# Rebuilding the stretch between a kernel's last lag products and its first feed-forward: first segments first, the first norm in halves, weights fetched apart

## The chip, the cores and the metric

One core of a Trainium2 chip runs the kernel. The metric is the device time of one execution in microseconds. The kernel before was timed three times: 1184.76, 1185.22 and 1189.84 us, median 1185.22 us.

## The reference, cut to what matters

Two layers, each a long convolution over time (a state-space model, S4) and a SwiGLU feed-forward part, each with a layer norm ahead of it and a residual around it. 2048 time steps, 512 channels, 128 states per channel, 1376 hidden columns, all in float32.

```python
def _A_ref(u, ...):                                  # the convolution
    P = jnp.exp(logdA[:, :, None] * l[None, None, :])
    K = jnp.einsum("dn,dnl,dn->dl", Cc, P, dB).real  # a kernel of 2048 lags for each channel
    ...                                              # y = K * u by FFT, + u * Dskip
def _B_ref(x, w_gate, w_up, w_down):
    g = _silu(x @ w_gate)
    u = x @ w_up
    return (g * u) @ w_down
x = A_u
x = x + _A_ref(_layernorm(x), ...)
x = x + _B_ref(_layernorm(x), ...)
x = x + _A_ref(_layernorm(x), ...)
x = x + _B_ref(_layernorm(x), ...)
```

## The kernel before, in words

Time is cut into four blocks of 512 steps. A block's convolution is done by transforms of short segments: the input block is turned into spectra in four groups of frequencies (`q`, in the order 0, 3, 1, 2, and in two halves `h` of 256 channels each), each spectrum is multiplied by the spectrum of a segment of the lags, products of earlier blocks with later segments are added up, and the result is turned back. The kernel runs in two stages.

**The lag kernel.** The lags are built for 64 channels at a time, in eight chunks. For a chunk the vector engine (DVE) builds tables of powers, TensorE (PE) multiplies them (`lags`, L510 and L511), spreads the result over the rows (`spread`, L526), and turns each of its four segments into spectra (`spectra`, matmuls on L547). Segment 0 alone goes into `w0r`, which stays in SBUF. Segments 1 to 3 need a sum of a segment with the other part of the one before (the wrap sums, tile `wo`) and go to DRAM (`wdr`). The wrap sums of chunks 0 to 5 are written on DVE (`wrapped`, L584 and L586), those of chunks 6 and 7 on GpSimd (POOL, L569, or L572 and L573 where segment 0 came ahead by itself).

**The blocks.** Then come eight pairs of a convolution (`ssm`) and a feed-forward part (`ffn`), in the order (layer, block) 00, 01, 02, 10, 03, 11, 12, 13. In an `ssm`, for each half and each `q`: the products (L762, and L765 adding the next one on), two rows that make a complex result of them (L766, L767), the inverse matmuls (L781, tile `pi`), `combine` (L742, L743), and after the four groups of a half fourteen rows of sums that add the result onto the block's rows `xt` (L796 to L811, many through the helper on L226). An `ffn` takes a block's 512 rows in two halves of 256. For each: the norm (`ffn_norm`), five groups of 256 columns of gate and up products (`pgu`, L886 to L888; SiLU on ScalarE (ACT), L891; product on DVE, L892; split into two f16 parts, L893 and L894), the last 96 columns (`remainder`, L853 to L855, on DVE L862 and L864), then the second product (`py`, L900 to L902), which DVE adds to the two rows of tiles (L905). So each half ends with two DVE rows on L905, the "adds"; the kernel has 32 of them. The norm of every half but the first ends in DVE rows on L839 (tile `nn`), and DMA transposes then bring it to PE.

All products of the feed-forward run with numbers split into two f16 parts, a high and a low one. So the f32 weights are split once: fetched, scaled and rounded to the high part on ACT (`hi`, L652 and L677), and the low part worked out on DVE (`lo`, L658 with 688 or 1376 columns a row, L680 with 512).

**The stretch between.** The change sits between the last chunk's `lags` and the first matmul of the first `ffn`. There the first convolution block has only one segment (`ssm(0, 0)`, generator `first`), its spectra of u wait in `u4`, and the first norm goes by a path of its own: bn_stats on DVE (L202, L203), four small POOL instructions (L204 to L207), a normalization on ACT (L825), eight PE transposes (L827), a high copy on ACT (L830) and a low part on DVE (L832).

What sets the order: the code of the lag kernel, through to the last weight split, stands in a `manual_schedule` block, which keeps PE, ACT and DVE in the order written among themselves. Code behind it (the other `ssm`s and `ffn`s) is placed by a list scheduler with priorities, and it may place later code among the rows of the block. Each engine then executes its own list strictly in order and waits at the first row whose input isn't there. SP issues the DMAs of the weights, of `wdr`, `udr` and the transposes, in order as well.

Of the kernel before, what the change touches and what calls it, by code (L numbers as in the profile page):

```python
# [12 lines left out]
F16 = mybir.dt.float16  # L13
# [3 lines left out]
OP = mybir.AluOpType  # L17
# [64 lines left out]
def kernel(ctx, tc, x, a_re, a_im, b_re, b_im, c_re, c_im, log_dt, d_skip,  # L82
# [449 lines left out]
    def spectra(ch, kt, k0, k1, qs=QORD, late=False):  # L532
# [4 lines left out]
        for q in qs:  # L537
            if k1 == 1:
                pw = pbig([P, 2, 8, 4, 16], "pw")[:, :, 0:1]
            elif k0 == 1:  # L540
                pw = pbig([P, 2, nk, 4, 16], "pw")
            else:
                pw = psml([P, 2, nk, 4, 16], "pw")
# [7 lines left out]
            if k1 == 1:  # L551
                A.activation(w0r[:, h, q, :, off:off + DC].rearrange("p i (g d) -> p i g d", g=4), pw[:, :, 0], AF.Copy)
                yield
                continue
            s1 = tl([P, 2, NB, 4, 16], "s1", "uu")
            A.activation(s1[:, :, :nk], pw, AF.Copy)
            if late:
                A.activation(w0r[:, h, q, :, off:off + DC].rearrange("p i (g d) -> p i g d", g=4), pw[:, :, 0], AF.Copy)
                wraps.append(wrapped(h, q, off, s1))
                yield  # L560
                continue
            if k0 == 0:
                G.tensor_copy(w0r[:, h, q, :, off:off + DC].rearrange("p i (g d) -> p i g d", g=4), s1[:, :, 0])
            sp, np_ = s1, NB - 1
            wo = tl([P, 2, NB - 1, 4, 16], "wo", "sg")
            ops = (OP.subtract, OP.add) if q % 2 == 0 else (OP.add, OP.subtract)
            for i in range(2):
                if k0 == 0:
                    G.tensor_tensor(wo[:, i], s1[:, i, 1:], s1[:, 1 - i, :3], ops[i])  # L569
                else:  # L570
                    w0s = w0r[:, h, q, 1 - i, off:off + DC].rearrange("p (g d) -> p g d", g=4)
                    G.tensor_tensor(wo[:, i, 0], s1[:, i, 0], w0s, ops[i])  # L572
                    G.tensor_tensor(wo[:, i, 1:], s1[:, i, 1:3], s1[:, 1 - i, :2], ops[i])  # L573
            for k in range(1, NB):
                nc.sync.dma_start(wdr[k, h, q, :, :, off:off + DC].rearrange("p i (g d) -> p i g d", g=4),
                                  wo[:, :, k - 1])
# [606 lines left out]
```

## Time and profile before

| what | value |
|---|---|
| median of three runs | 1185.22 us |
| the profiled execution's own time | 1189.7 us |
| its span | 1187.9 us |
| PE busy | 1108.9 us, 93% of the span |
| DVE busy | 1017.2 us, 86% |
| ACT busy | 621.3 us, 52% |
| POOL busy | 112.9 us, 10% |
| first matmul of the first feed-forward | 324.80 us |
| 2nd, 4th and 6th add (end of the first three halves' work) | 387.65, 446.57, 512.11 us |

"Busy" is the time in which an engine had an instruction under way; matmuls overlap one another, so a busy PE need not be one at its peak. Line numbers are those of the kernel before unless the text says otherwise; names of tiles stand in the form out<-in. The rows "waited for" give idle time of an engine just ahead of an instruction and what ended it. A column PEclk is the clock that TensorE was granted, 1.00 being full speed.

### The profile page before, as it was taken

How to read it: one execution, taken by the hardware profiler on the slowest of the kernel's cores; microseconds unless marked ns; L12 is line 12 of the kernel's file. 1: busy time of each engine (PE TensorE's matmuls, PEld its weight loads, DVE VectorE, ACT ScalarE, POOL GpSimd, SP SyncE). 2: the span in 40 equal slices, each digit the busy share in tenths (PEclk: the TensorE clock that was granted, in tenths of full speed). 3: DMA queues.
4: the chain of work that ended last, by engine and by line, in shares of the span. 5: the costliest groups of instructions: out<-in, count | busy, mean ns of one | idle time of the engine just before them, and what ended most of it. 6: DMA issues, size and time to landing. Idle time of an engine off the chain costs nothing.

```text
span 1187.9 us, 25243 instructions
## 1 busy us (share of the span) xinstructions
PE 1108.9 (93%) x10268; PEld 862.1 (73%) x10268; DVE 1017.2 (86%) x1669; ACT 621.3 (52%) x1190; POOL 112.9 (10%) x166
## 2 busy tenths in 40 slices
PE   2999899889789989899999999999999999999998
PEld 2867677677675848687768687858687686877875
DVE  8979999998899998999999999989992899983211
ACT  6999889862383553538553534735432452334211
POOL 3100200004200010001000100111000010000000
PEclk9989999999899989999999999989999999999999
DMA  6445455577695238332343444324534144312000
GB/s 235 124 139 127 119 124 124 128 191 197 193 282 170 76 115 200 114 103 83 103 151 122 121 167 144 105 77 155 153 105 135 45 121 134 120 41 46 14 23 18
DMA packets 138455, 146.90 MB, mean 124 GB/s; under 512 B 77858, under 2 KB 87074, under 8 KB 138339
## 3 DMA queue, kind: packets, MB, share of 16 engines
q1 hardware_dynamic: 133474, 128.51, 36.0%
q0 software_dynamic: 4864, 16.78, 6.1%
q8 instruction: 80, 1.31, 0.5%
q14 instruction: 37, 0.30, 0.1%
HBM read 98.19 MB, written 28.31 MB: 106 GB/s over the span
## 4 chain that ended last, share of the span: by engine, by line
PE 37%; DVE 24%; issue 4%; ACT 3%; DMA 3%; SPq 1%; POOL 1%; DVEq 0%; ACTq 0%; POOLq 0%
PE pgu L886 5%; PE pgu L887 5%; PE pgu L888 5%; PE py L900 5%; PE py L901 5%; PE py L902 4%; DVE t L762 4%; PE pi L781 3%; DVE yk L765 3%; PE pf L270 3%; DVE z L226 2%; DVE yk L762 2%; DMA mix<-nn 2%; DVE sg L892 2%; DVE hl L894 2%
## 5 line engine op out<-in xcount | busy, mean ns | idle before, releaser
L886 PE MATMUL pgu<-mix,wsl 128*128 128x256 f16 x1280 | 351.1, 274 | 4.6 <-DVE mix L832 2.4
L887 PE MATMUL pgu<-mix,wsl 128*128 128x256 f16 x1280 | 351.1, 274 | 0.0
L888 PE MATMUL pgu<-mix,wsl 128*128 128x256 f16 x1280 | 350.9, 274 | 0.0
L900 PE MATMUL py<-wsl,hh 128*128 128x512 f16 (+1 forms) x352 | 135.4, 385 | 9.3 <-DVE xg L905 4.7
L887 PEld LDWEIGHTS <-wsl 128*128 128x128 f16 x1280 | 125.9, 98 | 22.2 <-issue 5.9
L886 PEld LDWEIGHTS <-wsl 128*128 128x128 f16 x1280 | 126.0, 98 | 16.6 <-issue 0.3
L902 PE MATMUL py<-wsl,hl 128*128 128x512 f16 (+1 forms) x352 | 135.3, 384 | 2.7 <-DVE hl L894 2.7
L888 PEld LDWEIGHTS <-wsl 128*128 128x128 f16 x1280 | 126.0, 98 | 15.4
L901 PE MATMUL py<-wsl,hh 128*128 128x512 f16 x320 | 123.3, 385 | 0.0
L762 DVE TENSOR_TENSOR t<-uu,w 128x1024 f32<-128x1024 f32 x96 | 116.7, 1216 | 0.2
L765 DVE TENSOR_TENSOR yk<-yk,t 128x1024 f32<-128x1024 f32 x96 | 116.6, 1215 | 0.1
L891 ACT ACTIVATE sg<-pgu,sc 128x512 f32<-128x512 f32 x80 | 54.4, 680 | 106.5 <-PE pgu L888 100.2
L892 DVE SCALAR_TENSOR_TENSOR sg<-pgu,sc,sg 128x512 f32<-128x512 f32 x80 | 59.5, 744 | 50.6 <-ACT sg L891 50.4
L781 PE MATMUL pi<-yl,mix 128*128 128x256 f16 x672 | 91.6, 273 | 8.6 <-ACT yl L770 6.8
L547 PE MATMUL pw<-kt,ek 128*128 128x256 f32 (+2 forms) x420 | 95.9, 365 | 0.0
L893 ACT ACTIVATE hh<-sg 128x512 f16<-128x512 f32 x80 | 50.0, 626 | 78.5 <-DVE sg L892 78.3
L547 PEld LDWEIGHTS pw<-kt,ek 128*128 128x128 f32 x420 | 76.3, 190 | 9.1
L270 PE MATMUL pf<-z,eh 128*128 128x256 f16 x576 | 76.0, 273 | 0.0
L770 ACT ACTIVATE yl<-mix,sy 128x512 f16<-128x512 f32 x56 | 40.2, 718 | 64.5 <-DVE mix L767 64.3
L781 PEld LDWEIGHTS <-mix 128*128 128x128 f16 x672 | 65.1, 98 | 12.1 <-issue 2.2
L762 DVE TENSOR_TENSOR yk<-u,w0r 128x1024 f32<-128x1024 f32 x56 | 68.0, 1215 | 0.9 <-ACT u L272 0.9
L901 PEld LDWEIGHTS <-hh 128*128 128x128 f16 (+1 forms) x352 | 34.8, 99 | 46.4 <-issue 11.8
(247 smaller groups left out, 2182.9 us busy)
## 6 DMA issues: line engine op xcount, KB each, us to landing
w<-wdr SPq DMA_DIRECT2D x96, 256.0 KB, 2.7
uu<-udr SPq DMA_DIRECT2D x96, 256.0 KB, 3.0
udr<-u POOLq DMA_DIRECT2D x32, 256.0 KB, 2.5
wdr<-wo SPq DMA_DIRECT2D x96, 64.0 KB, 2.7
udr<-u SPq DMA_DIRECT2D x16, 256.0 KB, 2.2
g<-tmp POOLq DMA_DIRECT2D x8, 512.0 KB, 4.5
g<-btl POOLq DMA_DIRECT2D x8, 512.0 KB, 5.9
n<-xdr SPq DMA_DIRECT2D x4, 1024.0 KB, 5.6
```

Source lines behind the costliest of these rows:

```text
L270: PE.matmul(pf[:, o], lhsT=e, rhs=m, start=k == 0, stop=k == len(terms) - 1)
L547: PE.matmul(pw[:, i], lhsT=e, rhs=kt[:, :, c + 4 * k0:4 * k1:4, :].rearrange("p g k d -> p k g d"), start=c == 0, stop=c == 3)
L762: V.tensor_tensor(t, uu.unsqueeze(1).to_broadcast([P, 2, 2, HD]), w.unsqueeze(2).to_broadcast([P, 2, 2, HD]), OP.mult)
L765: V.tensor_tensor(yk, yk, t, OP.add)
L781: PE.matmul(pi[:, o], lhsT=e, rhs=m, start=k == 0, stop=k == len(terms) - 1)
L886: PE.matmul(o, lhsT=wgu(wi, k, 0)[:, fs], rhs=nh[:, k], start=k == 0, stop=False)
L887: PE.matmul(o, lhsT=wgu(wi, k, 0)[:, fs], rhs=nlo[:, k], start=False, stop=False)
L888: PE.matmul(o, lhsT=wgu(wi, k, 1)[:, fs], rhs=nh[:, k], start=False, stop=k == 3)
L892: V.scalar_tensor_tensor(sg, pgu[:, 1], sc6[:, 4:5], sg, OP.mult, OP.mult)
L900: PE.matmul(py[:, r], lhsT=hh[:n, f, rc], rhs=wd(f, 0)[:n], start=f == 0, stop=False)
L901: PE.matmul(py[:, r], lhsT=hh[:n, f, rc], rhs=wd(f, 1)[:n], start=False, stop=False)
L902: PE.matmul(py[:, r], lhsT=hl[:n, f, rc], rhs=wd(f, 0)[:n], start=False, stop=f == FT - 1)
```

## The change

Four things are rebuilt; the computation is the same.

- **First segments first.** Segment 0's spectra of the last two chunks, which the first convolution block needs, are taken ahead of everything else of these chunks: three groups of chunk 7 with 64 columns, and group 2 of both chunks at once with 128 (`firsts`). The segments 1 to 3 (`rest`: five groups, 192 columns) come later, partly behind the first norm's transposes. All wrap sums are on DVE now (L583, L585), none on POOL, and POOL's copies into `w0r` are ACT's.
- **The first block by itself.** `opening` replaces `ssm(0, 0)`: results, inverses, combines and the sums can be placed one at a time, the sums in three parts (first two output rows, third, fourth). The rows that the first norm doesn't need (third and fourth) come behind it.
- **The first norm in halves.** Statistics are taken on 256 columns of a half as soon as it is summed (L894); scale and offset are worked out on DVE, POOL does only the power (L900 of the change); one of the two rows is normalized on DVE (L905 of the change); transposes, high copies and low parts (L913 to L918) go in two pieces.
- **Weights fetched apart.** The DMA of a weight piece is no longer in its `hi`: a third list, `fetches`, starts them earlier, into more buffers (a tile `spare` in `W3`). w_down comes in pieces of three rows of tiles instead of four. Two pieces' high parts are on ACT before the first block is done.

The first steps of `ssm(0, 1)` are taken within the stretch, and the block with the order written out now ends ahead of the remaining splits, which the list scheduler places.

```diff
-    def ffn_norm(layer, b, s, wait=None):
...
+    def first_norm():
...
+        def half(h):
+            for r in range(rows):
+                V.bn_stats(st[:, r, h], xt[:, r, h * HD:(h + 1) * HD])
+        def scale():
+            for r in range(rows):
+                V.bn_aggr(mv[:, r], st[:, r])
+            V.tensor_scalar(rs[:, :rows], mv[:, :, 1], EPS, 1.0 / 256.0 ** 2, OP.add, OP.mult)
+            G.tensor_tensor(rs[:, :rows], rs[:, :rows], mhalf[:, :rows], OP.pow)
+        def normal():
+            V.scalar_tensor_tensor(nb[:, :rows], mv[:, :, 0], -1.0, rs[:, :rows], OP.mult, OP.mult)
+            A.activation(nn2[:, 0], xt[:, 0], AF.Identity, scale=rs[:, 0:1], bias=nb[:, 0:1])
+            V.tensor_scalar(nn2[:, 1], xt[:, 1], rs[:, 1:2], nb[:, 1:2], OP.mult, OP.add)
...
     spectra (...)
-            ops = (OP.subtract, OP.add) if q % 2 == 0 else (OP.add, OP.subtract)
-            for i in range(2):
-                if k0 == 0:
-                    G.tensor_tensor(wo[:, i], s1[:, i, 1:], s1[:, 1 - i, :3], ops[i])
-                else:
...
+            wraps.append(wrapped(h, q, off, s1, ("bb", "dd")[len(rests) % 2] if k0 else "sg"))
...
-        ready = ffn_norm(0, 0, 0, lambda: split(0, 2))
-        split(1, 0)
-        take(rest, 100)
-        split(1, 0)
-        take(first, 1)
-        split(0, 1)
-        while los:
-            split(1, 1) if his else split(0, 1)
...
+        result(7)
+        fetch(4)
+        for n in range(4, 8):
+            inverse(n)
...
+        sums1[0]()
+        half(1)
+        scale()
+        take(rest, 6)
...
+        normal()
+        flip(0)
+        flip(2)
+        split(2, 0)
+        ahead.append(next(spec))
+        second_block = ssm(*SEQ[1])
+        take(second_block, 1)
+        while wraps and len(wraps) > 3:
+            wrap()
+        sums0[1]()
+        low(0)
+        low(2)
+        split(0, 2)
+    split(2, 2)
+    fetch(2)
+    sums0[2]()
...
+        if k in (0, 2):
+            take(rest, 3)
...
```

How the rows move is seen in the order in which each engine gets its instructions. First PE, from the last spectra of the stretch to the first matmul of the feed-forward (`pw` are spectra of the lags, `pt` the transposed first rows, `pgu` the first feed-forward product). Before:

```order
L547 MATMUL pw<-kt_629,ef 128x192
L547 MATMUL pw<-kt_629,ek_85 128x192 x3
L827 MATMUL pt<-ident,nn_3422 128x128 x8
L886 LDWEIGHTS wsl_3116
L886 MATMUL pgu<-mix,wsl_3116 128x256
```

and now:

```order
L913 MATMUL pt<-ident,nn_3300 128x128 x8
L543 MATMUL pw<-kt_629,ef 128x192
L543 MATMUL pw<-kt_629,ek_84 128x192 x3
L543 MATMUL pw<-kt_629,ef 128x192
L543 MATMUL pw<-kt_629,ek_84 128x192 x3
L543 MATMUL pw<-kt_629,ef 128x192
L543 MATMUL pw<-kt_629,ek_85 128x192 x3
L543 MATMUL pw<-kt_629,ef 128x192
L543 MATMUL pw<-kt_629,ek_85 128x192 x3
L963 LDWEIGHTS wsl_3108
L963 MATMUL pgu<-mix,wsl_3108 128x256
```

Two groups of spectra, sixteen matmuls of 192 columns, now stand between the transposes and the feed-forward.

Second DVE, at the end of the first block's sums and the first statistics (`bn` rows; `wsl` is the split weights, `st` a fetched piece, `xg` the block's rows, `mix` on L832 the normed rows). Before:

```order
L202 BN_STATS st<-xg 128x6
L203 BN_AGGR mv<-st 128x2
L202 BN_STATS st<-xg 128x6
L203 BN_AGGR mv<-st 128x2
L658 SCALAR_TENSOR_TENSOR wsl_3116<-st_3301,sc_93,wsl_3116 128x2x344
L658 SCALAR_TENSOR_TENSOR wsl_3117<-st_3301,sc_93,wsl_3116 128x2x344
L658 SCALAR_TENSOR_TENSOR wsl_3118<-st_3304,sc_93,wsl_3117 128x4x344
L832 TENSOR_TENSOR mix<-pt,mix 128x1024
```

and now:

```order
L806 TENSOR_TENSOR t_3301<-t_3301,t_3302 128x256
L687 SCALAR_TENSOR_TENSOR wsl_3110<-st_3489,sc_93,wsl_3110 128x512
L226 SCALAR_TENSOR_TENSOR xg<-t_3301,xg 128x256
L894 BN_STATS st<-xg 128x6
L687 SCALAR_TENSOR_TENSOR wsl_3110<-st_3489,sc_93,wsl_3110 128x512
L894 BN_STATS st<-xg 128x6
L861 TENSOR_TENSOR dd_2915<-bb_2914,pi 128x512
L862 TENSOR_TENSOR bb_2914<-bb_2914,pi 128x512
```

Low parts of w_down (L687) now stand among the first half's sums, ahead of its statistics; they need the fetch of w_down and its high part. In all, from the end of the table building to the low part of the normed rows, the change has six split rows of 688 columns on DVE where before has two, two of 1376 where before has one, two of 512 where before has none, and ten wrap sums where before has none.

Third DVE around the 4th add, where the second half of the first feed-forward ends (L905 before, L982 now). Before, the normed rows `nn` (L839) of the next feed-forward are made at the 3rd add, well ahead of the 4th:

```order
L839 TENSOR_TENSOR nn_3422<-nn_3422 128x512
L226 SCALAR_TENSOR_TENSOR z_3524<-bt 128x256 x2
L905 SCALAR_TENSOR_TENSOR xg<-py,sc_93,xg 128x512
L226 SCALAR_TENSOR_TENSOR xg<-t_3844,xg 128x256
L226 SCALAR_TENSOR_TENSOR t_3845<-bb,dd 128x256
L765 TENSOR_TENSOR yk<-yk,t 128x1024
L226 SCALAR_TENSOR_TENSOR t_3844<-dd,bb 128x256
L839 TENSOR_TENSOR nn_3422<-nn_3422 128x512
```

and now, a piece that begins with the 4th add:

```order
L982 SCALAR_TENSOR_TENSOR xg<-py,sc_93,xg 128x512
L226 SCALAR_TENSOR_TENSOR z_3540<-z_3540 128x2x256
L762 TENSOR_TENSOR yk<-yk,t 128x1024
L226 SCALAR_TENSOR_TENSOR xg<-t_3859,xg 128x256
L812 TENSOR_TENSOR t_3868<-dd 128x256
L226 SCALAR_TENSOR_TENSOR z_3540<-bt 128x256 x2
L759 TENSOR_TENSOR t<-uu,w 128x1024
L226 SCALAR_TENSOR_TENSOR t_3873<-dd,bb 128x256
L813 TENSOR_TENSOR t_3867<-t_3867,t_3868 128x256
L762 TENSOR_TENSOR yk<-yk,t 128x1024
```

The last sums of block (0, 1) now follow the 4th add, and its normed rows (L877 now) come another nine and sixteen rows behind this piece:

```order
L877 TENSOR_TENSOR nn_3300<-nn_3300 128x512
L226 SCALAR_TENSOR_TENSOR yl_3541<-mix,sy,yl_3541 128x512
L226 SCALAR_TENSOR_TENSOR xg<-t_3873,xg 128x256
L762 TENSOR_TENSOR yk<-yk,t 128x1024
L226 SCALAR_TENSOR_TENSOR z_3540<-z_3540 128x2x256
L759 TENSOR_TENSOR t<-uu,w 128x1024
L226 SCALAR_TENSOR_TENSOR dd<-pi,sy,bb 128x512
L877 TENSOR_TENSOR nn_3300<-nn_3300 128x512
```

Of DVE's rows between the 2nd and the 4th add, the change has fewer than before (1 product, 3 additions of products, 2 `z` and 1 low part of it, 9 sums, 1 low part `yl`, 2 `nn`, 2 of the remainder), and between the 4th and the 6th more (4 products, 5 additions, 2 rows of results, 8 sums, 1 `yl`, 2 `nn`).

More of the change, by code (lines that the diff above doesn't have):

```diff
@@ L1076 @@
         spec, ahead = inputs(), []
-        first = ssm(0, 0)
+        result, inverse, combine, total = opening()
         sp = spectra(i, kt, 0, NB, QORD[:3])
@@ L1110 @@
         scales()
-        take(first, 2)
-        load_x(xs[0], 0, 0)
+        kp = spread(i, ks)
+        inverse(1)
+        combine(0)
+        split(1, 0)
+        A.activation(kts[1], kp, AF.Copy)
+        result(2)
+        wrap()
+        wrap()
+        result(3)
+        sp = itertools.chain(spectra(i, kts[1], 0, 1, QORD[:3]), firsts(i - 1, kt2, QORD[3]))
+        rest = itertools.chain(spectra(i - 1, kts[0], 1, NB, QORD[3:]), spectra(i, kts[1], 1, NB))
+        split(0, 1)
         take(sp, 2)
-        take(first, 2)
```

295 lines of the change are left out of this document (184 added, 111 removed).

## The prediction

> **What bounds the kernel now.** I read the page's busy time first, then the busy time of each engine in five stretches: from the end of the last chunk's tables to the first feed-forward matmul, then to the 2nd, the 4th and the 6th add, then the rest. One more stretch, the first 5.2 us of the feed-forward, comes from a call of its own.
>
> ```profile
> PE 1108.9 (93%) x10268; PEld 862.1 (73%) x10268; DVE 1017.2 (86%) x1669; ACT 621.3 (52%) x1190; POOL 112.9 (10%) x166
> ...
> core 0: us, PE busy (x) PEld busy (x) DVE busy (x) ACT busy (x) POOL busy (x), PEclk, DMA share, GB/s
> 271.00:324.80 53.80, 45.88 (x505) 39.28 (x504) 42.92 (x84) 15.63 (x23) 17.91 (x27) 0.95 0.62 188
> 324.80:387.70 62.90, 56.92 (x456) 42.35 (x456) 62.10 (x88) 37.06 (x64) 4.55 (x7) 0.91 0.74 226
> 387.70:446.60 58.90, 54.01 (x406) 39.63 (x405) 55.90 (x105) 30.52 (x59) 6.90 (x7) 0.94 0.31 96
> 446.60:512.10 65.50, 60.96 (x547) 48.25 (x544) 61.32 (x100) 29.89 (x57) 4.45 (x7) 1.00 0.57 153
> 512.10:1187.90 675.80, 660.06 (x5513) 508.71 (x5510) 544.15 (x897) 282.25 (x544) 41.60 (x52) 0.99 0.33 100
> ```
>
> ```profile
> 324.80:330.00 5.20, 5.20 (x27) 3.65 (x27) 5.03 (x10) 3.83 (x7) 1.98 (x4) 0.53 0.65 209
> ```
>
> From 512 us on PE is the bound: it lacks 15.7 us in 676. Ahead of that DVE is as full as PE or fuller: from 324.80 to 387.70 it lacks 0.8 us, to the 4th add 3.0, to the 6th 4.2, 8.0 in all. In the stretch that the change rebuilds neither is full (PE lacks 7.9 us, DVE 10.9). What stands still there is in the waits of that stretch and in its last links in order of time:
>
> ```profile
> PE pt L827 <- ACT nn L825: 4.6, 1, 4.6
> PE pgu L886 <- DVE mix L832: 2.4, 1, 2.4
> ...
> DVE mix L832 <- ACT mix L830: 4.3, 1, 4.3
> DVE dd L742 <- PE pi L781: 3.2, 2, 2.0
> DVE xg L797 <- DMA xg<-in_A_u_dram: 1.3, 1, 1.3
> ```
>
> ```profile
> 315.77 0.18 DVE L203 BATCH_NORM_AGGREGATE mv<-st 128x2 f32<-128x6 f32 x1
> ...
> 316.05 0.78 POOL L204 TENSOR_SCALAR rs<-mv 128x2 f32<-128x2 f32 x1 [0.42 <-DVE mv L203]
> 316.91 1.29 POOL L205 TENSOR_TENSOR rs<-rs,mhalf 128x2 f32<-128x2 f32 x1
> ...
> 319.32 0.24 POOL L207 TENSOR_SCALAR rs<-rs 128x2 f32<-128x2 f32 x1
> 319.59 1.52 ACT L825 ACTIVATE nn<-xg,rs 128x512 f32<-128x512 f32 x2 [5.71 <-POOL rs L207]
> ...
> 320.46 1.97 PE L827 MATMUL pt<-ident,nn 128*128 128x128 f32 x8 [4.58 <-ACT nn L825]
> ...
> 322.46 1.02 ACT L830 ACTIVATE mix<-pt 128x1024 f16<-128x1024 f32 x1 [1.35 <-PE pt L827]
> ...
> 323.52 1.22 DVE L832 TENSOR_TENSOR mix<-pt,mix 128x1024 f16<-128x1024 f32 x1 [4.34 <-ACT mix L830]
> ```
>
> The norm is a chain through four engines: 3.5 us of small POOL instructions, then ACT, PE, ACT, DVE. PE stands 4.6 us for it and 2.4 us more for its end, and the granted clock in the 5.2 us behind is 0.53, a loss of 0.47 × 5.2 = 2.4 us.
>
> The Trainium skill ("TensorE: Matmul & The Clock Gate", Part 1: The HAM clock gate) says that an idle window of about 3.4 us halves the clock and about 3.4 us of sustained work brings it back; the 4.58 us wait and the 0.53 behind it agree.
>
> **The change part by part.** It is priced with these rows (the addition L765 is taken as long as the product L762; it has the same operands' size):
>
> ```profile
> L762 DVE TENSOR_TENSOR t<-uu,w 128x1024 f32<-128x1024 f32 x7 | 8.5, 1216 | 0.0
> ...
> L680 DVE SCALAR_TENSOR_TENSOR wsl<-st,sc,wsl 128x512 f16<-128x512 f32 x10 | 6.8, 741 | 0.0
> L658 DVE SCALAR_TENSOR_TENSOR wsl<-st,sc,wsl 128x1376 f16<-128x1376 f32 x4 | 6.6, 1644 | 0.0
> L658 DVE SCALAR_TENSOR_TENSOR wsl<-st,sc,wsl 128x688 f16<-128x688 f32 x6 | 5.3, 922 | 0.0
> L226 DVE SCALAR_TENSOR_TENSOR yl<-mix,sy,yl 128x512 f16<-128x512 f32 x6 | 4.5, 742 | 0.0
> L767 DVE TENSOR_TENSOR yf<-yk 128x256 f32<-128x256 f32 x8 | 4.2, 521 | 0.0
> ...
> L226 DVE SCALAR_TENSOR_TENSOR xg<-t,xg 128x256 f32<-128x256 f32 x6 | 3.0, 492 | 0.2
> ...
> L767 DVE TENSOR_TENSOR mix<-yk 128x256 f32<-128x256 f32 x6 | 2.5, 417 | 0.0
> ...
> L839 DVE TENSOR_TENSOR nn<-nn 128x512 f16<-128x512 f32 x2 | 1.4, 680 | 0.0
> ```
>
> ```profile
> L584 DVE TENSOR_TENSOR wo<-s x24: 339/351/360, 89.4 to 260.4; 128x192 f32<-128x192 f32 x24
> ```
>
> ```profile
> L547 PE MATMUL pw<-kt,ek 128*128 128x192 f32 x36 | 6.8, 326 | 0.0
> ```
>
> *Stretch, DVE up to the low part of the normed rows* (before, it ends at 323.52 + 1.22 = 324.74). Added rows: four splits of 688 (3.7 us), one of 1376 (1.6), two of 512 (1.5), ten wrap sums (3.5), a normalized row like L839 (0.7), small ones (0.2); three sums go behind it (-1.3). That is +9.9. Taken away: the waits, 4.3 + 3.2 + 1.3 = 8.8, since splits and results of other groups now stand between a combine and its inverse, between the norm's links and ahead of the transfer. POOL's work leaves too. The same row L767 took 0.52 us here and 0.42 later, while POOL was at work for 17.9 us in the stretch; that row's excess alone is 8 × 0.10 = 0.8, and the same 0.10 on all 84 rows would be 8.4. I take 3, nearer the row that shows it, as longer rows lose little. New waits: between 1.4 (two combines that still stand right behind their inverses, at about 0.7 each, the length of a row of 512 columns) and 4 (the norm's links, when the rows placed between them don't cover). Sum: 9.9 - 8.8 - 3 + (1.4 to 4) = -0.5 to +2.1; I take +0.3, so the low part ends at 325.
>
> The Trainium skill ("SBUF — State Buffer", Who interferes with whom) has a rule for this: a DVE instruction with two SBUF inputs and a GpSimd instruction that reads SBUF exclude each other for the whole instruction. The 0.52 against 0.42 agrees in kind; by full exclusion the upper 8.4 would be the relief and the total some 5 us lower, 1183; I give that 1 in 10, inside the chance of my forecast.
>
> *Stretch, PE.* The norm's chain loses three POOL steps (3.5 us to about 1.3), but between statistics and low part DVE's order now has a split of 1376 (1.6), a normalized row (0.7), a product (1.2), eight wrap sums (2.8), five sums (2.2) and small rows (1.1), together 9.6 us, so the statistics are done about 325 - 9.6 - 1.2 = 314, the transposes about 320.5, and then come the two groups of spectra, 16 × 0.326 = 5.2 us: the feed-forward starts at about 325.5, 0.7 us later than before. The spectra were ahead of the transposes and are no new work; they fill the wait that let the clock fall, and the first feed-forward matmuls run at full clock: -2.4. Whether the spectra themselves are slowed costs 0 to 2.4, and shows only if it passes the low part's end; I take it as hidden by DVE.
>
> *To the 2nd add.* DVE had 62.10 busy of 62.90. Counted in the order, all rows from the tables to the 2nd add are 4.3 us more (sixteen wraps 5.6, sums, remainder and norm 1.9; two products and two result rows fewer, -3.2); as 9.9 of additions lie ahead of the low part, 5.6 go from this stretch: 56.5. PE needs 56.9 - 2.4, and 24 forward matmuls of it are now later. With 1.5 us of waits 58 us: the 2nd add at 383.5, 4.1 earlier.
>
> *To the 4th add.* The order has DVE rows fewer: 4 products and additions (4.9), 9 sums (4.1), 2 `nn` (1.4), `z`, `yl` and remainder (2.7): 13.1, times 0.93 because rows overlap by some 0.08 us, so 12.2; 55.9 - 12.2 = 43.7. Now PE bounds it: 54.0 less the 24 forward matmuls that now come behind it (2.6), and 3 of its 4.9 us of waits: 54.4. The 4th add at 437.9, 8.7 earlier. But DVE, strictly in order, stands for about 10 us here that it cannot use.
>
> *To the 6th add.* Here the rows come back: 9 products and additions (10.9), 2 result rows (0.8), 8 sums (3.6), `yl` (0.7), 2 `nn` (1.4): 17.5 × 0.93 = 16.3. 61.32 + 16.3 = 77.6, and 2 us of waits (4.2 before): 79.6, against 65.5 before. The 6th add at 517.5, 5.4 us later. The place where it shows is this one, where the next feed-forward half began 3 us behind the 4th add:
>
> ```profile
> 446.57 0.75 DVE L905 SCALAR_TENSOR_TENSOR xg<-py,sc,xg 128x512 f32<-128x512 f32 x1 [2.09 <-PE py L902]
> ...
> 449.33 0.21 PE L854 MATMUL pgu<-wsl,mix 128*128 128x96 f16 x1
> ```
>
> Now the two `nn` rows stand 18 and 25 rows behind that add with the last sums of block (0, 1) ahead of them, about 17 us of DVE by the lengths above, and PE has only forward and inverse matmuls meanwhile.
>
> *The rest.* PE's matmuls are the same to the end, so its lateness is carried; DVE has 3.4 us less than before there (+5.0 over all, +8.4 by the 6th add), and of PE's 15.7 us of waits I take 2 as given back. Net +3.4 us. The profiled execution took 1189.7 us around a span of 1187.9, 4.5 above the median; the sum by it is 1193.1, and on the median of 1185.2 it is **1188.6 us**.
>
> Costed at nothing: ACT's copies into `w0r` (ACT is busy 15.6 of 53.8 us), and the extra DMA descriptors of smaller w_down pieces (DMA share 0.62 in the stretch).
>
> **The rivals.** *Faster:* DVE stays the limit to the 6th add and waits no more than the 8.0 us of before. Then its rows decide alone: +8.4 - 8.8 - 3 = -3.4 at the 6th add, -5.4 with the same 2 us given back, 1179.8. For it speaks that DVE lacked 0.8 us only in the first of these stretches, against it that between the 2nd and 4th add it falls to 43.7 of work while PE needs over 51. It decides if DVE's waits from the feed-forward's start to the 6th add stay under 8 us; I reckon 13.
>
> *Slower:* weights late. Two w_down low parts stand in DVE's list ahead of the first statistics; their fetch goes out only when an earlier piece's buffer is read, and all behind it waits. A fetch of this size takes about 7 us:
>
> ```profile
> st<-in_B_w_up_dram SPq DMA_DIRECT2D x3, 688.0 KB, 7.2
> ```
>
> By the order it is issued some 6 to 8 us of DVE rows ahead of its reader, which costs 0 to 1.3 in my sum; with a busy queue and ACT's high part behind others half a landing, 3.6 us, is lost. All later adds shift by it: 1192.2, and 1196 if the whole landing shows.
>
> *No change of speed:* the feed-forward starts where it did, and what DVE saves to the 4th add it repays by the 6th exactly: 1185.2.
>
> **How the numbers follow.** My forecast, between 1183 and 1194 by its own bounds (waits of the stretch -0.8 to +1.8, waits to the 6th add 4 us either way), has 0.45, the faster rival 0.25, late weights 0.2, no change 0.1. A measurement of this kernel tells about 0.5% (5.9 us) from no change. Faster by more: nearly all of the faster rival that falls below 1179.3 or close to it, 0.22, and 0.02 of mine. Slower by more, above 1191.1: 0.18 of late weights and 0.10 of mine. Within: 0.48. The range reaches below the faster rival's 1179.8, as the relief from POOL may be more than 3, and to the dearer end of late weights: 1178 to 1196.
>
> **What would show it.** Right: the feed-forward's first matmul at 324 to 327, at full clock, with spectra ahead of it; POOL nearly empty in the stretch; the 4th add 6 to 10 us earlier, and the 6th add 2 to 8 us later; `nn` rows of the second block 15 us or more behind the 4th add; PE's longest waits there. Wrong: a first matmul at 320 or before, or a 6th add before 512; then the DVE order didn't bind. A DVE wait on a weight split in the stretch points to late weights.

## The result, and the profile after

The change takes 1195.3 us in the median (five of six executions between 1193.2 and 1197.1; the sixth took 4040.7, which nothing here explains). The six executions of before that stand beside it had a median of 1185.1 us. The medians are 10.2 us apart. The ratio on record is 1.0062, with a 95% interval of 1.0037 to 1.0088: slower by 4.4 to 10.4 us, so the gap between the medians lies near the upper end of what the runs allow. The profiled execution took 1195.1 us around a span of 1193.2, 5.3 us more than the profiled one of before.

The busy times of the change in the same stretches as before, cut at its own first feed-forward matmul and its own 2nd, 4th and 6th add (columns: from and to, length, then busy of PE, PE's weight loads, DVE, ACT, POOL, then granted clock, DMA share and GB/s):

```profile
core 0: us, PE busy (x) PEld busy (x) DVE busy (x) ACT busy (x) POOL busy (x), PEclk, DMA share, GB/s
271.00:327.58 56.58, 49.20 (x530) 43.84 (x529) 48.31 (x105) 24.52 (x40) 0.72 (x1) 0.94 0.66 221
327.58:384.64 57.06, 52.86 (x459) 40.17 (x457) 53.41 (x87) 25.84 (x45) 1.10 (x3) 0.97 0.67 207
384.64:436.97 52.33, 49.51 (x388) 37.77 (x387) 45.15 (x83) 24.79 (x50) 2.94 (x5) 1.00 0.23 76
436.97:515.33 78.36, 66.56 (x557) 51.22 (x556) 77.05 (x125) 38.76 (x77) 7.70 (x9) 0.89 0.52 155
515.33:1193.20 677.87, 659.91 (x5517) 508.50 (x5514) 543.42 (x897) 284.26 (x544) 42.18 (x52) 1.00 0.33 99
```

The 2nd add is 3.0 us earlier than before, the 4th 9.6 us earlier, the 6th 3.2 us later, the last 5.4 us later. The loss to the 6th add is in one stretch: from the 4th to the 6th add PE lacks 11.8 us (4.5 before) at a clock of 0.89, and DVE is full: it lacks 1.3 us of 78.4. Its normed rows (`nn`) stand there, 11.4 and 16.5 us behind the add:

```profile
436.97 0.74 DVE L982 SCALAR_TENSOR_TENSOR xg<-py,sc,xg 128x512 f32<-128x512 f32 x1
...
448.37 0.68 DVE L877 TENSOR_TENSOR nn<-nn 128x512 f16<-128x512 f32 x1
...
453.50 0.68 DVE L877 TENSOR_TENSOR nn<-nn 128x512 f16<-128x512 f32 x1
```

and PE's longest waits there are for what DVE makes late (ACT's `yl` comes from DVE's result rows `mix`, which stand behind the sums):

```profile
PE pi L780 <- ACT yl L769: 7.5, 1, 7.5
...
PE pgu L932 <- DMA mix<-nn: 3.0, 2, 2.9
...
ACT yl L769 <- DVE mix L766: 2.8, 2, 2.4
```

In the stretch itself, the timeline from the low part of the normed rows to the first feed-forward matmul, and the clock in four windows from the transposes on (columns as above):

```profile
318.84 1.97 PE L913 MATMUL pt<-ident,nn 128*128 128x128 f32 x8 [2.38 <-ACT nn L904]
...
320.60 0.85 PE L543 MATMUL pw<-kt,ef 128*128 128x192 f32 x2
...
323.51 1.28 DVE L918 TENSOR_TENSOR mix<-pt,mix 128x512 f16<-128x512 f32 x2
...
327.58 0.38 PE L963 MATMUL pgu<-mix,wsl 128*128 128x256 f16 x2
```

```profile
318.80:320.60 1.80, 1.76 (x9) 1.77 (x9) 1.80 (x5) 0.60 (x1) 0.00 (x0) 0.50 0.00 0
320.60:324.00 3.40, 3.40 (x12) 3.40 (x12) 3.40 (x13) 3.16 (x4) 0.00 (x0) 0.50 0.66 156
324.00:327.58 3.58, 3.58 (x23) 3.52 (x22) 3.58 (x8) 0.98 (x4) 0.00 (x0) 0.97 0.48 104
327.58:333.00 5.42, 5.42 (x52) 4.87 (x50) 3.35 (x10) 2.44 (x4) 0.00 (x0) 1.00 0.78 232
```

The low part ended at 324.79, and PE was still at the spectra, which ran at half clock to 324 and took 7.0 us: the start is theirs. DVE's waits in the stretch did not go; others took their place, 7.1 us in place of 8.8:

```profile
DVE wsl L663 <- ACT wsl L658: 3.2, 2, 3.0
DVE yk L837 <- ACT w0r L548: 2.1, 2, 1.5
DVE bb L861 <- PE pi L850: 1.1, 1, 1.1
DVE wsl L687 <- ACT wsl L684: 0.7, 1, 0.7
```

### The profile page after: what moved, and what is told of

Read it like the earlier page. It is cut to its first block, busy times and chain, and to the rows that moved or that the text cites. A ratio compares the mean times of both kernels' runs of the same rounds, so it can differ in the third digit from the quotient of the medians.

```text
span 1193.2 us, 25270 instructions
## 1 busy us (share of the span) xinstructions
PE 1105.6 (93%) x10284; PEld 863.7 (72%) x10284; DVE 1019.3 (85%) x1691; ACT 623.9 (52%) x1199; POOL 87.3 (7%) x136
## 4 chain that ended last, share of the span: by engine, by line
PE 41%; DVE 35%; ACT 9%; issue 8%; DMA 5%; POOL 1%; SPq 1%; DVEq 0%; ACTq 0%; POOLq 0%
PE pgu L963 6%; PE pgu L964 6%; PE pgu L965 6%; DVE t L759 4%; PE py L977 3%; PE pi L780 3%; DVE yk L762 3%; PE py L978 3%; PE py L979 3%; DVE z L226 2%; PE pf L270 2%; DVE yk L759 2%; PE pw L543 2%; DVE sg L969 2%; DMA mix<-nn 1%
## 5 line engine op out<-in xcount | busy, mean ns | idle before, releaser
L780 PE MATMUL pi<-yl,mix 128*128 128x256 f16 x672 | 93.9, 277 | 13.7 <-ACT yl L769 9.4
L270 PEld LDWEIGHTS <-eh 128*128 128x128 f16 x576 | 56.8, 99 | 19.2 <-issue 10.0
L971 DVE TENSOR_TENSOR hl<-sg,hh 128x512 f16<-128x512 f32 x80 | 54.8, 685 | 14.8 <-ACT hh L970 14.5
```

The costliest lines, as they stand in the source:

```text
L270: PE.matmul(pf[:, o], lhsT=e, rhs=m, start=k == 0, stop=k == len(terms) - 1)
L780: PE.matmul(pi[:, o], lhsT=e, rhs=m, start=k == 0, stop=k == len(terms) - 1)
```

## The experiments

Twelve runs were made, one of them of the kernel before as it stands. What follows names each, quotes what was expected (with a "theory" and a "rival" that forecast different times), and gives its median time. The interval in the table is against executions of before that were timed beside it; as their medians went from 1186 to 1189 us, a few microseconds between two medians of different experiments say little by themselves. One lesson belongs ahead of them, as the expectations were written before it was seen: the traces part already ahead of the stretch. The last table rows of the lag kernel (tile `re`, work that neither the change nor an edit touches) end between 269.1 and 273.6 us in the fourteen traces:

```profile
268.80 2.29 DVE L459 TENSOR_TENSOR re<-re,mu 128x992 f32<-128x992 f32 x2
```

```profile
271.31 2.28 DVE L459 TENSOR_TENSOR re<-re,mu 128x992 f32<-128x992 f32 x2
```

```profile
267.72 2.28 DVE L459 TENSOR_TENSOR re<-re,mu 128x992 f32<-128x992 f32 x2
```

These are before, before in a second trace, and the change: ends at 271.1, 273.6 and 270.0. So add times are compared from that end. The table has them so, with the DVE rows that stand ahead of the 6th add beyond those of before. They are counted in the traces from the tables' end on, each at its net length (from its start to that of a row right behind it, the median over all traces: 0.27 us for a wrap sum, 1.14 for a product):

| kernel | DVE rows ahead of the 6th add, us more than before | tables end | 6th add, from there | last add, from there | time against before, 95% interval |
|---|---|---|---|---|---|
| before | 0 | 271.1 | 241.0 | 912.7 | |
| before_again | 0 | 273.6 | 236.2 | 907.4 | |
| the change | 7.2 | 270.0 | 245.3 | 919.2 | 1.0037 to 1.0088 |
| ffn_first | 7.9 | 269.5 | 246.5 | 930.6 | 1.0160 to 1.0213 |
| rest8 | 9.1 | 270.8 | 248.2 | 921.4 | 1.0066 to 1.0128 |
| late_second | 9.1 | 272.0 | 247.6 | 919.9 | 1.0052 to 1.0111 |
| rest8_late | 0.5 | 273.4 | 241.4 | 912.4 | 0.9985 to 1.0026 |
| manual_all | 1.1 | 270.2 | 240.8 | 911.6 | 0.9991 to 1.0033 |
| manual_part | 0.5 | 271.2 | 241.3 | 914.0 | 1.0013 to 1.0047 |
| manual_late | 1.1 | 269.1 | 241.2 | 911.4 | 0.9996 to 1.0027 |
| manual_late_norm | 0.5 | 272.8 | 241.3 | 911.7 | 1.0006 to 1.0048 |
| wraps_pool | 5.4 | 271.4 | 255.3 | 925.8 | 1.0103 to 1.0147 |
| before_auto | 2.3 | 269.2 | 244.4 | 913.3 | 1.0003 to 1.0039 |
| before_wraps_dve | 13.1 | 271.8 | 255.1 | 919.1 | 1.0063 to 1.0107 |

**Before, once more.** Unedited.

> The kernel before, unedited, for a second trace. Of its six executions shown so far two took 1189.8 us and four 1184.3 to 1185.2, and the profiled one is a slow one. If the 4.7 us are one place (a transfer that lands late at one add), the add times of this trace part from the first one's at that place. If they are spread, or the execution is again one of 1189.8, nothing parts. It tells how much of the 10 us between the medians lies outside the two traces, which differ by 5.3 us in their spans.

One execution, 1186.9 us. From the tables' end its 6th add is 4.8 us nearer than in the first trace (236.2 against 241.0), 1.5 of that by the feed-forward's start, 3.0 by the 4th add; behind the 6th add the two run alike (671.2 and 671.7 us to the last). So the profiled execution on which the prediction built was a long one, and a good part of the gap between medians that the traces don't show lies there. What made those 4.8 us was not found.

**Priority for the first feed-forward groups.**

```diff
                         o = pgu[:, wi, i]
+                        with tc.high_priority(offset=BOOST if ready and s == 0 and f0 < 4 else 0):
...
```

> The change with one edit: the first two groups of gate and up products of the first feed-forward get priority, so that they stand among the last spectra on PE. All work is the same, the wrap sums stay on DVE. By the order, two of the nn rows of the second block now stand ahead of the 4th add (none in the change), and DVE's rows between the 4th and 6th add fall by some 12 us, those ahead of the 4th rise by as much. Theory (the order of DVE's rows around the 4th add makes PE wait): the 4th add at 441 to 445, later than the change's 437.0, the 6th at 507 to 511 instead of 515.3, PE's waits between them back from 11.8 us to 3 to 5, and the time 4 to 8 us below the change's, 1187 to 1191 on the median. Rival (DVE's amount of work to the 6th add, +7 us with the wrap sums, decides whatever the order): the 6th add within 1.5 us of 515.3 and the time within 2 us of the change's.

1209.6 us, 14 us above the change: neither theory had the time. Up to the 6th add the rival was right. The order did what was meant (4th add 448.7, 67.3 us from it to the 6th, PE lacking 5.2 there), but the 6th add came at 516.0, 0.6 us from the change's: what DVE does ahead of an add it does not do behind it. Then 12 us were lost between the 6th and the 8th add (74.1 us, 61.9 in the change). PE lacks 5.3 us there, 4.4 of it in order behind forward matmuls that waited for DVE (the change has no such wait there), and it has more matmuls in this stretch at a clock of 0.95; what else the order moved was not followed up:

```profile
448.68:515.96 67.28, 62.07 (x528) 47.47 (x526) 64.22 (x102) 31.71 (x63) 6.41 (x8) 0.95 0.53 155
515.96:590.09 74.13, 68.84 (x562) 53.80 (x561) 63.90 (x132) 44.95 (x90) 7.49 (x12) 0.95 0.24 76
```

```profile
PE pf L270 <- DVE z L226: 4.4, 2, 2.6
```

**Wrap sums of the last two chunks on POOL.**

```diff
-        V.tensor_tensor(wo[:, 0], s1[:, 0, 1:], s1[:, 1, :3], ops[0])
+        E = G if h == 1 and off >= 2 * DC else V
+        E.tensor_tensor(wo[:, 0], s1[:, 0, 1:], s1[:, 1, :3], ops[0])
```

> The change with one edit: the sixteen wrap sums of the last two chunks on POOL again instead of DVE (5.6 us by their length on DVE). By the order, one nn row of the second block moves ahead of the 4th add and DVE's rows between the 4th and 6th fall by some 5 us. Rival (amount of DVE work decides): the 6th add 4 to 6 us earlier, 509 to 511, and the time 4 to 6 us lower. Theory (order): only as far as the nn rows move, PE's waits between the 4th and 6th add 8 to 10 us instead of 11.8, time 1 to 3 us lower. If POOL's sums slow DVE's rows as they did before (0.52 against 0.42 us on L767), the first feed-forward starts 1 to 3 us later than in the change.

1203.1 us, 8 us above the change; both theories fell. Sixteen rows left DVE, yet from the tables' end to the 6th add it was busy 228.4 us where the change has 224.9, though it has 1.8 us fewer rows there. So the rows beside POOL's sums grew by some 5.3 us, where the sixteen sums take 4.3 net on DVE itself. The same row of 256 columns takes 0.42 us alone:

```profile
327.31 0.76 DVE L766 TENSOR_TENSOR mix<-yk 128x256 f32<-128x256 f32 x1
...
338.21 0.81 DVE L821 TENSOR_TENSOR t<-t,t 128x256 f32<-128x256 f32 x1
```

**The kernel before with its wrap sums on DVE.**

```diff
-                    G.tensor_tensor(wo[:, i], s1[:, i, 1:], s1[:, 1 - i, :3], ops[i])
+                    V.tensor_tensor(wo[:, i], s1[:, i, 1:], s1[:, 1 - i, :3], ops[i])
```

(and so in the two lines of the other branch).

> The kernel before with one part of the change alone: the wrap sums of chunks 6 and 7 on DVE instead of POOL, at the same places. Rival (amount of DVE work): DVE has 6 to 8 us more to the 6th add, which comes 4 to 8 us later, and the time is 3 to 7 us above before. Theory (order): the order keeps three nn rows of the second block ahead of the 4th add, so the 4th to 6th add stays at 64 to 66 us; the sums cost only where they stand, 0 to 3 us in all.

1198.0 us, 9 us above before, and the 6th add 14 us later: both past the rival's ranges, and far past the theory's. It is no clean test of amount, for at their old places the sums made DVE wait 13.4 us (the `wo` lines), with all else queued behind:

```profile
DVE wo L569 <- ACT s L556: 5.8, 1, 5.8
DVE wo L569 <- DMA wdr<-wo: 5.6, 1, 5.6
DVE mix L832 <- ACT mix L830: 4.3, 1, 4.3
DVE wo L572 <- ACT s L556: 2.0, 1, 2.0
```

The change takes them up later, out of a list, and in its stretch DVE has no wait on them (its waits are listed above).

**One group of spectra ahead of the transposes.**

```diff
-        take(rest, 6)
+        take(rest, 8)
         pscale = product_scale()
```

> The change with one edit: the spectra matmuls of the fourth late group stand ahead of the first norm's transposes on PE instead of behind, so one group instead of two lies between transposes and feed-forward. DVE's order up to the 4th add is that of the change, row for row but for a few. In the change the feed-forward's first matmul came at 327.58, 2.8 us behind the low part of the normed rows (324.79). Theory (PE's spectra hold the start, DVE's time holds the 6th add): the first matmul at 324.5 to 325.5, the first add 1.5 to 2.5 us earlier, the 4th by 0 to 2, the 6th within 1.5 us of 515.3, and the time within 3 us of the change's. Rival (the late start is carried through to the end): all adds and the time 2 to 2.8 us earlier.

1198.2 us. The feed-forward began at 322.8, earlier than expected, and then PE waited 1.5 us for the low part and 4.4 us for PSUM that DVE's SiLU products free:

```profile
PE pgu L963 <- DVE sg L969: 4.4, 2, 3.7
PE pgu L964 <- DVE mix L918: 1.5, 1, 1.5
```

From the tables' end the first add came at 104.5 us (104.2 in the change): an earlier start by 5.6 us was worth nothing 50 us later, which speaks against the rival. The 6th add was 2.9 us later than the change's, outside the theory's 1.5. The order has one product and two result rows more (1.8 us) ahead of that add, which the expectation had passed over as "a few".

**The first product of block (0, 1) not taken in the stretch.**

```diff
-        ahead.append(next(spec))
-        second_block = ssm(*SEQ[1])
-        take(second_block, 1)
...
+            if i == 0:
+                ahead.append(next(spec))
```

> The change with one part undone: the first product of block (0, 1) is not taken within the stretch. Behind the 4th add its order is that of the kernel with the fourth late group moved, so the two share whatever the later order costs. Theory: to the 6th add within 1.5 us of the change, since DVE's amount to there is the same; behind it the two kernels run alike, and part from the change's add times by the same amounts at the same adds. Rival (each start difference is carried to the end): they differ at the end by what they differ at the first add.

1196.7 us. The 6th add 2.3 us later than the change's from the tables' end, with the same 1.8 us of rows more ahead of it as in rest8, so the 1.5 us were missed again and for the same reason. The second half held: from the 6th to the 22nd add these two kernels, whose DVE rows there stand in the same order to the last one, stay within 0.6 us of each other at every add, though their feed-forwards began 7.6 us apart on the clock.

**The order of the remaining splits written out.** The lines from `split(2, 2)` to the end of the loop over `los` stand in the `manual_schedule` block again, as they stood before.

> The change with one part undone: the remaining weight splits, late wrap sums and sums stand inside the part with the order written out, as before, instead of being placed by the list scheduler. By the order DVE has 8 to 9 us fewer rows ahead of the low part of the normed rows (no hoisted splits). Theory: the low part ends at 318 to 321, the feed-forward starts with the last spectra out of the way at 321 to 324, but DVE's amount to the 6th add is 6 us less by the order's count, so the 6th add is 4 to 8 us earlier than 515.3, and the time 0 to 6 us below the change's. Rival (the high parts on ACT bound the first half, DVE's hoisted splits cost nothing): first add no earlier than 374, and the time within 2 us of the change's or above.

1188.1 us, no longer to be told from before, and 7 us below the change by the medians, 6 by the two ratios to before (1.0012 and 1.0062); the intervals of the two do not touch. The feed-forward began at 317.3, before the expected 321 to 324. The 6th add came at 511.0 as expected, with PE's wait behind the 4th add as large as in the change or larger (14.4 us of 78.9):

```profile
271.00:317.29 46.29, 43.60 (x515) 38.72 (x514) 38.27 (x84) 16.65 (x31) 0.72 (x1) 1.00 0.63 208
317.29:382.70 65.41, 55.84 (x462) 42.83 (x461) 60.32 (x101) 32.98 (x55) 1.32 (x3) 0.95 0.71 216
382.70:432.16 49.46, 49.08 (x386) 37.42 (x384) 42.14 (x75) 21.31 (x44) 2.12 (x3) 1.00 0.21 67
432.16:511.02 78.86, 64.50 (x555) 50.39 (x554) 77.91 (x127) 38.09 (x77) 8.63 (x11) 0.91 0.54 160
```

From the tables' end to the 6th add DVE is busy 219.4 us where the change has 224.9. The fall in time is at the end of the theory's range or just past it, and the rival's first add (374 or later) came at 373.1.

**Both small edits at once** (`rest, 8` and the late first product).

> The change with both edits at once, the fourth late group's spectra ahead of the transposes and the first product of block (0, 1) not taken in the stretch. Its order behind the 4th add is one of its own: some 8 us fewer DVE rows from the 4th to the 6th add than in the change, 10 of them behind. Theory (DVE's time to the 6th add): by the order's count the 6th add comes 6 to 8 us earlier, 507 to 510, and PE's waits from the 4th to the 6th fall from 11.8 to 5 to 8 us; what it does behind is not fixed by that. Rival: as the two edits alone, within 3 us of the change.

1187.5 us, while with each edit alone the median stood 1.4 and 2.9 us above the change's (their intervals overlap the change's, so neither is shown to be slower). The 6th add at 514.8 on the clock missed the expected 507 to 510; from the tables' end, which came at 273.4, it is 241.4, 3.9 us nearer than the change's. PE lacks 9.3 us behind the 4th add (5 to 8 expected). That two edits gain together where neither gains alone speaks against pricing them one by one: the rows ahead of the 6th add, 9.1 us beyond before with either edit, are 0.5 beyond it with both.

**One part of the change put into the kernel before.** Everything from the first `split(1, 0)` behind the first norm stands outside the block with the written order.

> The kernel before with one part of the change alone: the weight splits and late spectra that follow the first norm stand behind the part with the order written out, so that the list scheduler places them. By the order some 9 us of splits and sums come ahead of the low part of the normed rows, and to the 6th add DVE has one product and one addition more (2.3 us). The wrap sums stay on POOL. Theory (rows that the list scheduler draws ahead of the 6th add lengthen DVE's time to it, and this is most of what the change costs): the feed-forward starts 5 to 9 us later than 324.8, the first add is 3 to 7 us later, the 6th at 512 to 516 (509.8 and 512.1 in the two traces of before), and the time 2 to 6 us above before. Rival (the cost comes from the rest of the change, its first block and norm): within 2 us of before.

1190.7 us against 1187.1, a ratio of 1.0021. The feed-forward started at 334.8, 10 us later (5 to 9 expected), the first add came 13.7 later (3 to 7 expected), and the 6th at 513.6 as expected; 2.5 us were left at the end. The interval, 0.4 to 4.6 us, takes in the rival's 2, so a loss from this part is likely in the kernel before too, but the run does not settle it; it is smaller than the 6 to 7 us that the change gains by undoing the like part (manual_all).

**Half of the splits written out** (the block ends ahead of `k = 0`, the loop stays outside).

> The change with half of the undone part: two weight pieces, the late wrap sums and the first block's last sums stand inside the part with the order written out, the other splits and the last two groups of spectra are left to the list scheduler. By the order DVE has 7 us fewer rows ahead of the low part than in the change, and 6 to 7 us fewer to the 6th add, as many as with everything written out. Theory (rows ahead of the 6th add): the 6th add at 509 to 512.5 as with everything written out (511.0), the time within 3 us of that kernel's 1188.1. Rival (what helped there was the order of the last splits): 6th add at 514 or later, the time within 3 us of the change's 1195.3.

1191.0 us, within 3 us of the kernel with everything written out; 6th add at 512.5, the end of the range.

**Everything written out, and the late first product.**

> The change with the splits' order written out again, and the first product of block (0, 1) not taken in the stretch. DVE's rows to the 6th add are in sum those of the kernel with everything written out; three fewer microseconds of them stand between the 4th and the 6th add, four more ahead. Theory (the sum to the 6th add decides, how it is dealt out around the 4th doesn't): 4th add 2 to 5 us later than that kernel's 432.2, 6th add at 509.5 to 512.5, time within 2.5 us of 1188.1. Rival (the wait of PE behind the 4th add decides): 6th add 3 us earlier or more, time at or below 1184.

1188.6 us, 6th add at 510.4, both as expected; the 4th add came 1.5 us later than the parent's, not 2 to 5. The window from the 4th to the 6th add shows what the rival would have needed: PE lacks 9.6 us to the 6th add, 4.8 less than its parent, and the 6th add from the tables' end is the same (241.2 and 240.8).

```profile
433.67:510.36 76.69, 67.08 (x568) 52.66 (x566) 74.48 (x119) 34.95 (x69) 7.34 (x11) 0.91 0.52 157
```

**The norm's scale on POOL again**, in the kernel just above (manual_late).

```diff
-            V.tensor_scalar(rs[:, :rows], mv[:, :, 1], EPS, 1.0 / 256.0 ** 2, OP.add, OP.mult)
+            G.tensor_scalar(rs[:, :rows], mv[:, :, 1], EPS, 1.0 / 256.0 ** 2, OP.add, OP.mult)
...
-            V.tensor_scalar(nn2[:, 1], xt[:, 1], rs[:, 1:2], nb[:, 1:2], OP.mult, OP.add)
+            A.activation(nn2[:, 1], xt[:, 1], AF.Identity, scale=rs[:, 1:2], bias=nb[:, 1:2])
```

> The kernel with the order written out and the late first product, with one part of the change undone: the first norm's scale and offset on POOL in four steps and both rows normalized on ACT, as before; statistics, transposes and low parts stay in halves. DVE's rows to the 6th add are 0.3 us fewer. In its parent the aggregate came at 309.17, the transposes at 312.70, the feed-forward at 316.23. Theory (the norm's chain sets the feed-forward's start, DVE's sum sets the 6th add): transposes and feed-forward 2 to 4 us later, the 6th add within 1.5 us of 510.4, the time within 2.5 us of 1188.6. Rival (the start of the feed-forward is carried to the end): 6th add and time 2 to 4 us later.

1190.4 us, 1.8 above its parent. The 6th add came at 514.1 on the clock, as the rival had it; but the aggregate was already 3.6 us late (312.80 against 309.17), and the tables with it. From their end the feed-forward starts 2.9 us later, as expected, the 6th add 0.1 us later, and the last 0.3. The norm's chain moves the start, and the start isn't what the 6th add waits for.

None of these kernels is faster than before beyond its interval.

## Why the prediction was right, and where its size was not

The sign was right, and so was the main step: DVE bounds the kernel up to the 6th add, its rows there drain late, and the 6th add comes later. The size was short: +3.4 forecast against +4.4 to +10.4. That 1195.3 us lies within the stated range is luck: the forecast's own upper bound was 1194, and the range reached to 1196 only for late weights, which is not what happened. Of the chances, 0.28 lay on a time above 1191.1. One link of the mechanism was taken for more than it is: PE's wait for the `nn` rows behind the 4th add is there, but by the later runs it is not what holds the 6th add.

- *The start.* Forecast 325.5, found 327.58. The low part's time was right (325, found 324.79), but by errors that cancel. Counted from the tables' end it came 1.2 us later than in the first trace of before: the rows added are 8.6 us net (9.9 forecast), POOL's leaving gave 4.9 (3 forecast), and DVE's idle time fell by 2.6 (6.6 forecast, 8.8 of waits less 2.2 of new ones). Mis-sized was "I take it as hidden by DVE" for spectra at half clock: 5.2 us forecast, 7.0 found, and they held the start. The 2.4 us of clock were gained in the feed-forward and paid in the transposes and spectra (5.2 us at 0.50). Later runs suggest that this term is idle: rest8 started 5.6 us earlier, counted from the tables' end, and had its first add where the change had it.
- *The waits.* The step "8.8 taken away, 1.4 to 4 new" failed: 7.1 are new. The prediction gave a DVE wait on a weight split as the sign of late weights, and the longest one, 3.0 us, is just that; but the sign misleads here. The piece was issued at 270.0 and landed 4.9 us later. ACT came to its high part only at 282.3, in order behind the copy of the last lag products and an inverse's result, for which it had waited:

```profile
279.84 1.02 ACT L516 ACTIVATE ks<-pk 128x1024 f32<-128x1024 f32 x1 [4.57 <-PE pk L511]
281.77 0.60 ACT L858 ACTIVATE bb<-pi 128x512 f32<-128x512 f32 x1 [0.90 <-PE pi L850]
282.26 1.43 ACT L658 ACTIVATE wsl<-st,sc 128x1376 f16<-128x1376 f32 x1
```

  Weights that landed late show in two places, 3.5 us of ACT's time for w_down and 1.6 for a piece of w_gate, but only 0.7 and 0.2 of it reached DVE. The rest (`yk`, `bb`) is the way from the last lag products over ACT, PE and ACT to `w0r` and from the inverses back. DVE reaches a split or a result early and stands there instead.
- *POOL.* Relief was put at 3. Rows ahead of the 6th add grew by 7.2 us (8.4 forecast), yet DVE's busy time from the tables' end to it only from 222.2 to 224.9. So some 4.5 us came from rows that no longer run beside POOL, and by the same count 3.4 to 5.0 in all nine kernels that have the sums on DVE in the change's manner; the row that had 0.52 us is back at 0.42:

```profile
L842 DVE TENSOR_TENSOR yf<-yk 128x256 f32<-128x256 f32 x8 | 3.3, 418 | 0.0
```

The Trainium skill ("SBUF — State Buffer", Who interferes with whom) has a DVE instruction with two SBUF inputs and a GpSimd instruction that reads SBUF shut each other out; both this and the 0.81 us rows above agree in kind.
- *The adds.* 2nd: -4.1 forecast, -3.0 found; 4th: -8.7 and -9.6; 6th: +5.4 and +3.2 on the clock. DVE from the 4th to the 6th add: 77.6 and 77.05 busy. The `nn` rows, forecast 15 us or more behind the 4th add, stood 11.4 and 16.5 behind, and the feed-forward's start, 324 to 327 by the signs, at 327.6. DVE's waits from the start to the 6th add: 13 forecast, 12.1 found, so the faster rival, with its bound of 8, was out.
- *The rest.* The step "of PE's 15.7 us of waits 2 are given back" failed in sign: PE lacks 18.0 us behind the 6th add, and the change loses 2.2 there.
- *The base.* The sum was made against one long execution and put on the median as it stood. The change's executions lie close to its profiled one (1195.1, median 1195.3), those of before do not (1189.7, median 1185.1). Of the 10.2 us between medians the traces show 5.3.

What the runs put in place of "nn behind the 4th add makes PE wait" is wider: in the nine kernels with the wrap sums on DVE in the change's manner, the 6th add follows DVE's rows ahead of it and little else. With 0.5 to 1.1 us of rows beyond before it stands at 240.8 to 241.4 us from the tables' end, with 7.2 to 9.1 at 245.3 to 248.2, whatever PE's wait behind the 4th add (5.2 to 14.4 us) and the feed-forward's start (46 to 58 us). DVE's busy time over the same way says it again: 217.8 to 219.4 us in the first five, 224.9 to 226.5 in the other four, and its idle time is 20.4 to 23.6 in all nine. Before, the change, and the change with everything written out, from the tables' end to the 6th add:

```profile
271.09:512.11 241.02, 217.69 (x1906) 169.44 (x1905) 222.15 (x372) 113.09 (x201) 33.72 (x48) 0.95 0.56 166
```

```profile
269.99:515.33 245.34, 218.85 (x1931) 173.47 (x1930) 224.92 (x396) 114.74 (x213) 12.47 (x18) 0.94 0.53 166
```

```profile
270.21:511.02 240.81, 213.52 (x1913) 169.65 (x1912) 219.43 (x383) 109.83 (x207) 12.78 (x18) 0.96 0.54 166
```

The change's share in it is that its last splits, sums and spectra are dealt out by the list scheduler: with them written out, 6.2 us of rows (three products, six rows `bt`, two `z` and a small one) no longer come ahead of that add, which does not need them, and the time falls from 1195.3 to 1188.1. What the change rebuilds otherwise then gains nothing that the runs show either: its feed-forward starts 47.1 us behind the tables, where before it starts at 53.7 and 52.2, and the time is that of before (1.0012, 0.9991 to 1.0033). That the undone part costs the time is shown by that run; that the rows are the way in which it does is shown by counts and nine traces that agree, not by taking them away alone, as every edit moved other rows too. What the order does behind the 6th add (12 us in ffn_first, 2 in the change) stays open.

What the weights fetched apart do by themselves is not shown: no run undoes that part alone.

## What to carry to other kernels

Where one engine is full to a certain point, count the rows that stand ahead of that point on it. Here an earlier start elsewhere, or a wait removed, came back as a later wait, while rows of later work drawn ahead moved that point by most of their length. If a list scheduler deals out part of the order, a small edit can change rows a long way behind it, so judge it by the whole order and not by the edited place. And when a measured time lands in your range, ask which term brought it there. Line two traces up at the last work that both share, and take a second trace of the kernel before: here executions of the same code part by several microseconds ahead of the place in question.

## What the runs showed of the hardware

- The end of work that no edit touches scattered over 4.5 us (269.1 to 273.6) between executions.
- Waits of little over 2 us were followed by half clock in some places and not in others; the length of one wait alone doesn't tell. In the change PE waited 2.2 us, did one small matmul, and waited 2.4; the clock was 0.50 from 318.8 to 324.0. With the splits written out PE waited 1.5 us before the transposes and the clock stayed at 1.00.

```profile
PE pt L913 <- ACT nn L904: 2.4, 1, 2.4
PE pm L609 <- DVE wmax L607: 2.2, 1, 2.2
```

  In late_second a single wait of 2.1 us was followed by 3.4 us at 0.50:

```profile
306.65 1.33 PE L850 MATMUL pi<-yf,mix 128*128 128x256 f32 x3 [2.06 <-DVE yf L841]
```

```profile
306.95:310.35 3.40, 3.40 (x10) 2.74 (x9) 3.37 (x7) 1.78 (x3) 0.00 (x0) 0.50 1.07 395
```

  In rest8_late one of 2.3 us left the clock at 1.00:

```profile
321.76 0.98 PE L913 MATMUL pt<-ident,nn 128*128 128x128 f32 x7 [2.29 <-ACT nn L904]
```

```profile
321.76:327.00 5.24, 4.87 (x35) 4.52 (x36) 5.24 (x19) 4.54 (x8) 0.00 (x0) 1.00 0.35 77
```

- Sixteen wrap sums on POOL, 0.6 to 1.85 us each, cost DVE some 5.3 us in longer rows beside them; on DVE itself they take 0.35 us each and 4.3 net in all.
